# Decode attention with a gated MLP: the output row in two PSUM banks, and the loads of K and wo without the order behind the last round's arm

## The chip, the cores and the metric

The kernel runs on one core of a Trainium2 chip. Five engines work side by side, each with its own queue of instructions: TensorE (PE; its weight loads are shown as PEld), VectorE (DVE), ScalarE (ACT), GpSimd (POOL) and SyncE (SP), which here issues nearly all transfers. Sixteen DMA engines carry the transfers. The metric is the device time of one execution, in microseconds (us).

## The reference

Two sequences, one new token each (`B = 2`, `Sq = 1`, `D = 1024`). `A` is attention with 32 heads over a cache of 16384 positions, `B` a small MLP block, and a gate mixes the two:

```python
g = sigmoid((x * gate_w).sum(-1, keepdims=True))
a = A(x, k_cache, v_cache, wq, wo)   # q = x@wq; softmax(q.k / sqrt(128)); o = p@v; o@wo
b = B(x, w1, w2, w3, w4)             # x1 = x + shifted(gelu(ln(x)@w1))@w2; x1 + gelu(ln(x1)@w3)@w4
return g * a + (1 - g) * b           # B's x is A's x
```

With one token a sequence the shifted parts are all zero, so `x1` is `x`. The caches are bf16, [2, 32, 16384, 128] each: 268 MB of K and 268 MB of V, read once. All the weights together are some 35 MB.

## The kernel before

**Memory.** One big tile `mem` in SBUF has five cells of 4.19 MB. A block of K or V is two heads of one sequence, 8.39 MB, and takes two cells. `K_CELL = (0, 1)`: K of sequence 0 lies in cells 0 and 1, K of sequence 1 in cells 1 and 2, so that the two share cell 1. Therefore `score_first` (four transposes, L423, and their score matmuls, L429) works on the half in cell 1, after which the other sequence's K may be loaded over it, and `score_second` on the other half. V goes to cells 3 and 4 (`V_CELL = 3`), and there is a single place for it. `wo_pair` holds the 256 rows of wo that belong to two heads (0.52 MB).

**Order.** There are 16 pairs of heads. The work on one pair and one sequence `b` is a unit: transposes of K on VectorE (L423), score matmuls (L429), a softmax in two parts (`softmax_a`, `softmax_b`), the product with V (`pv`, L483) and its end (`pv_end`), and after both sequences `project`, which multiplies by `wo_pair` (L375). Units are staggered: the scores of one unit run ahead of the product of the one before. One round of the hardware loop (L600, 15 rounds) is `odd_rest(i)` and then `even_unit(i + 1)`. After it comes an `If` that only the last round takes, with `last_unit`: the last V, the last wo, the last weight w4 in four pieces, and the output.

The loads stand on SyncE in this order in every round: wo (L367) and K of sequence 0 for the next pair (L112), V of sequence 1 (L115), K of sequence 1 (L112), V of sequence 0 (L115). A load is issued when what it overwrites has been read: K of sequence 0 after `score_second(0)` (cell 0) and after `score_first(hp, 1)` (cell 1), the last work on VectorE in a round. The order of instructions within an engine is fixed by `in_order`, which ties each to the one before; waits between engines and on transfers are placed by the tile layer from what reads and writes the same memory, and across the rounds of the loop too. `wo_pair` is read by `project` in `even_unit` and again by `project` in `last_unit`.

**The `If`.** An engine that does not take the arm goes through another one (its rows have L604), in which its semaphores are moved on by as much as the arm would have moved them. Before it adds to a semaphore it waits until that has its value of this round. SyncE's own arm of that kind thus waits for the loads of the round that share semaphores with `last_unit`'s loads; the latest of them is K of sequence 1.

**The output.** All products that end in the output row are added up in one PSUM tile `arow`: quarter `g` of the 1024 columns stands on partitions 32g and 32g + 1, 256 columns wide. Three functions add into it: `mlp_residual` (once, ahead of the loop), `project` (each round) and `mlp_last` (L403, at the very end, four pieces of w4). `write_out` copies quarters 0 and 2 with VectorE (L524) and 1 and 3 with ScalarE (L526) into `out_row`, and SyncE stores it (L527).

Of the kernel before, what the change touches and what calls it, by code (L numbers as in the profile page):

```python
# [10 lines left out]
FP32 = mybir.dt.float32  # L11
# [12 lines left out]
def kernel(  # L24
# [15 lines left out]
    nc = tc.nc  # L40
    P = nc.NUM_PARTITIONS
    B, Sq, D = A_x.shape
    _, H, Sk, Dh = A_k_cache.shape
# [3 lines left out]
    KC = D // P  # L47
# [6 lines left out]
    NJ = 2 * Sk // P  # L54
# [5 lines left out]
    QP = P // Q4  # L60
    CELL = NJ * Dh // 2
    G1 = D // Q4
# [8 lines left out]
    ops = ctx.enter_context(tc.tile_pool(name="ops", bufs=1, space=PSUM))  # L71
# [8 lines left out]
    def region(cell, elements, offset=0):  # L80
        at = cell * CELL + offset
        return mem[:, at : at + elements]
# [21 lines left out]
    K_CELL = (0, 1)  # L104
    V_CELL = 3

    def cache_rows(cache, hp, b):
        two = cache[b, bass.ds(2 * hp, 2)]
        return two.rearrange("h s d -> (h s) d").rearrange("(p j) d -> p (j d)", p=P)

    def load_k(hp, b):
        nc.sync.dma_start(out=region(K_CELL[b], NJ * Dh), in_=cache_rows(A_k_cache, hp, b))  # L112

    def load_v(hp, b, cell=V_CELL):
        nc.sync.dma_start(out=region(cell, NJ * Dh), in_=cache_rows(A_v_cache, hp, b))  # L115
# [6 lines left out]
        out=ident_s[:], in0=ident_f[:], scalar1=-scale, scalar2=None, op0=ALU.mult  # L122
# [10 lines left out]
        out=mask4[:], in_=mask4[:], compare_op=ALU.is_ge, fill=0.0,  # L133
# [3 lines left out]
        out=mask4[:], in_=mask4[:], compare_op=ALU.is_ge, fill=0.0,  # L137
# [11 lines left out]
        out=lmat[:].rearrange("p (g h k) -> p g h k", h=2, k=4),  # L149
        in_=hm2[:].unsqueeze(1).unsqueeze(3).to_broadcast([P, P // 8, 2, 4]),  # L150
# [5 lines left out]
        out=lane[:],  # L156
        in_=ident_f[:].rearrange("p (c k) -> p k c", k=QP),
# [5 lines left out]
    for g in range(Q4):  # L163
        nc.vector.tensor_scalar(
            out=spread[:, g],
# [2 lines left out]
        )  # L168

    oacc = [ops.tile([P, 4 * Dh], FP32, name=f"oacc{k}") for k in range(2)]  # L170
    arow = ops.tile([P, G1], FP32, name="arow")
    S_tiles = [ops.tile([P, GT * QP], FP32, name=f"S{k}") for k in range(2)]
    for t in (oacc[0], oacc[1], arow):
        nc.vector.memset(t[:], 0.0)

    WW = P + NG
# [2 lines left out]
    for k in range(2):  # L179
        t = const.tile([P, 4, WW], BF16, name=f"qw{k}")  # L180
        nc.gpsimd.memset(t[:], 0.0)
        qw.append(t)
        t = const.tile([P, NJ // 4, 2, 4], BF16, name=f"pt{k}")
# [17 lines left out]
    def turned(wide, C):  # L201
        t = mlp.tile([P, C, QP], FP32, tag="turn", name="turn")
        nc.vector.transpose(  # L203
            out=t[:].rearrange("p c k -> p (c k)"), in_=wide.rearrange("p c k -> p (c k)")
        )
        return t[:, :, 0:B]
# [86 lines left out]
    def spread_batch(t, C):  # L293
        return t[:].unsqueeze(1).to_broadcast([P, C, B])
# [31 lines left out]
    for k in range(2):  # L326
        wide = mlp.tile([P, 16, QP], FP32, tag="wide", name="wide")
        nc.scalar.activation(  # L328
            out=wide[:].rearrange("p (c e) i -> p c e i", e=2),
            in_=oacc[k][:].rearrange("p (c i e) -> p c e i", i=QP, e=2),  # L330
            func=ACTF.Copy,
        )
        t = turned(wide[:], 16).rearrange("p (x a v) b -> p a x b v", x=2, a=2)
# [12 lines left out]
    for e in range(2):  # L346
        half = slice(e * HALF, (e + 1) * HALF)
        nc.vector.tensor_copy(
            out=qdu[half].rearrange("p u v -> p (u v)"),
            in_=qdps[half, e].rearrange("p k g n -> p (k g n)"),  # L350
# [13 lines left out]

    def load_wo(hp):
        rows = A_wo[bass.ds(hp * 2 * Dh, 2 * Dh)]
        nc.sync.dma_start(  # L367
            out=wo_pair[:].rearrange("p t n -> p (t n)"),
            in_=rows.rearrange("(p t) n -> p (t n)", p=P),
        )  # L370

    def project():
        for t in range(2):
            for g in range(Q4):
                nc.tensor.matmul(  # L375
                    arow[QP * g : QP * g + B, :],
                    lhsT=oT[:, t, :],
                    rhs=wo_pair[:, t, g * G1 : (g + 1) * G1],
                    start=False,
                    stop=False,  # L380
                    skip_group_check=True,
                )

    def mlp_residual():
        x1g = mlp.tile([P, KC, B], FP32, name="x1g")
        nc.vector.tensor_tensor(
            out=x1g[:], in0=x1T[:], in1=spread_batch(omg, KC), op=ALU.mult
        )
        for r in range(KC):
            for g in range(Q4):  # L390
                nc.tensor.matmul(
                    arow[QP * g : QP * g + B, :].rearrange("b (i r) -> b r i", r=KC)[:, r, :],
                    lhsT=x1g[:, r, :],
                    rhs=ident_f[:, QP * g : QP * (g + 1)],
                    start=(r == 0),
                    stop=False,
                    skip_group_check=True,
                )

    def mlp_last(w4):  # L400
        for r in range(FC):
            for g in range(Q4):
                nc.tensor.matmul(  # L403
                    arow[QP * g : QP * g + B, :],
                    lhsT=h2T[:, r, :],
                    rhs=w4[:, r, g * G1 : (g + 1) * G1],
                    start=False,
                    stop=(r == FC - 1),
                    skip_group_check=True,
                )  # L410
# [29 lines left out]
    def score_first(hp, b):  # L440
        write_qw(hp, b)
        score_chunks(b, halves[1 - b], True, False)

    def score_second(b):
        score_chunks(b, halves[b], False, True)

    def softmax_a(b):
        S = S_tiles[b]
        st = ppool.tile([P, GT, QP], FP32, name="St")
        nc.vector.transpose(out=st[:].rearrange("p j r -> p (j r)"), in_=S[:])  # L450
        m = stat.tile([P, 1], FP32, name="m")
        nc.vector.tensor_reduce(out=m[:], in_=st[:, :, 0:NG], axis=AX.XY, op=ALU.max)  # L452
        Dm = ppool.tile([P, P], FP32, name="Dm")
        nc.scalar.activation(out=Dm[:], in_=ident_s[:], func=ACTF.Copy, scale=m[:, 0:1])  # L454
        st_tiles[b] = (st, Dm)
# [23 lines left out]
    def pv(b, cell=V_CELL):  # L479
        V = view(cell)  # L480
        for g in range(NJ // 4):
            q = g % Q4
            nc.tensor.matmul(  # L483
                oacc[b][QP * q : QP * q + 8, :],
                lhsT=pts[b][:, g].rearrange("p h k -> p (h k)"),
                rhs=V[:, 4 * g : 4 * g + 4, :].rearrange("p j d -> p (j d)"),
                start=(g < Q4),
                stop=(g >= NJ // 4 - Q4),
            )
# [4 lines left out]
    def pv_end(b):  # L494
        osb = ppool.tile([P, 4 * Dh], FP32, name="osb")
        nc.scalar.activation(  # L496
            out=osb[:], in_=oacc[b][:], func=ACTF.Copy, scale=rinvs[b][:, 0:1]
        )
        lines = osb[:].rearrange("p (k d t) -> p k t d", k=4, t=2)
        ot = misc_psum([P, 2])  # L500
        for t in range(2):
            for k in range(4):
                for h in range(2):
                    nc.tensor.matmul(  # L504
                        ot[h * HALF : (h + 1) * HALF, t : t + 1],
                        lhsT=lines[:, k, t, :],
                        rhs=lane[:, k + 4 * h : k + 4 * h + 1],
                        start=(k == 0 and t == 0),
                        stop=(k == 3),
                        skip_group_check=True,  # L510
                    )
        nc.vector.tensor_scalar(  # L512
            out=oT[:, :, b], in0=ot[:], scalar1=g_rep[:, b : b + 1], scalar2=None, op0=ALU.mult
        )
# [4 lines left out]
    def write_out():  # L519
        for g in range(Q4):  # L520
            at = out_row[:, g * G1 : (g + 1) * G1]
            row = arow[QP * g : QP * g + B, :]
            if g % 2 == 0:
                nc.vector.tensor_copy(out=at, in_=row)  # L524
            else:
                nc.scalar.activation(out=at, in_=row, func=ACTF.Copy)  # L526
        nc.sync.dma_start(out=out.rearrange("b s n -> (b s) n"), in_=out_row[:])  # L527


    load_k(0, 0)  # L530
    w3 = load_weight(B_w3, 3)
    compute_gate()
    mlp_residual()


# [6 lines left out]
    softmax_b(0)  # L542
    score_first(0, 1)

    def odd_rest(hp):
        load_wo(hp)
        load_k(hp + 1, 0)
        score_second(1)
        softmax_a(1)
        pv(0)  # L550
        load_v(hp, 1)
        pv_end(0)
        softmax_b(1)

    def even_unit(hp):
        score_first(hp, 0)
        load_k(hp, 1)
        score_second(0)
        softmax_a(0)
        pv(1)  # L560
        load_v(hp, 0)
        pv_end(1)
        project()
        softmax_b(0)
        score_first(hp, 1)
# [34 lines left out]
    with tc.For_i(0, HP - 1, 1, iteration_sync="reg_based") as i:  # L600
# [3 lines left out]
        with tc.If(i >= HP - 2):  # L604
            last_unit(HP - 1)
            in_order()


# [1 line left out]
_INS = ['A_x', 'A_k_cache', 'A_v_cache', 'A_wq', 'A_wo', 'B_x', 'B_w1', 'B_w2', 'B_w3', 'B_w4', 'gate_w']  # L610
# [26 lines left out]
```

## Time and profile before

| | us |
|---|---|
| median of 3 runs | 1337.62 (1336.85 to 1338.44) |
| the profiled execution | 1337.09 |
| its span, first to last instruction | 1334.9 |
| busy: PE / PEld / DVE / ACT / POOL | 772.2 / 335.1 / 652.4 / 130.4 / 12.9 |
| moved by the transfers | 572.68 MB, 429 GB/s over the span |

The page of the profile gives the span, the busy time of each engine and the share of the DMA engines in 40 slices; the trace behind it tells when each instruction ran, what it had waited for, and when transfers were issued. A row of the timeline has the start in us, the duration, the engine and line, the operation, its tiles and how many were merged, and in brackets the idle time before it and what ended that. `SPq`, `PEq` and the like are the queues of the engines, where branches, waits and issues are seen.

### The profile page before, as it was taken

Reading aid. Unit: us, or ns where it says so; the run is one execution under the profiler, and the core shown is the slowest. Engines: PE = TensorE matmul, PEld = TensorE weight load, DVE = VectorE, ACT = ScalarE, POOL = GpSimd, SP = SyncE. Lnnn points to the kernel's source line nnn. Section 1 sums busy time; section 2 is a strip of 40 time slices with the busy share of each in tenths; the row PEclk is TensorE's granted clock in tenths of the full one; section 3 lists DMA queues with packets and bytes.
Section 4 is the critical chain, followed back from the end, with each engine's and each line's share of the span. In section 5 each row is a group of like instructions: output and inputs, shape, how many; then the busy total and the mean of one; then the engine's idle time right before and its main releaser. Section 6 shows DMA issues by size and latency. Waiting matters only on the chain. (4 is left out here: it accounts for less than half of the span.)

```text
span 1334.9 us, 14766 instructions
## 1 busy us (share of the span) xinstructions
PE 772.2 (58%) x5758; PEld 335.1 (25%) x5758; DVE 652.4 (49%) x510; ACT 130.4 (10%) x204; POOL 12.9 (1%) x47
## 2 busy tenths in 40 slices
PE   1554657455566545567555556655556765655763
PEld 1222223222222222222222222222222222222322
DVE  2454455444455544445553445555444555544550
ACT  0011101111110111110011111001111000111110
POOL 1000000000000000000000000000000000000000
PEclk9677878777888777788777788877778876778886
DMA  9999999999999999999999999999999999999997
GB/s 409 436 434 427 438 405 440 416 448 438 426 440 424 440 438 426 438 426 440 424 440 438 426 438 426 440 424 440 438 426 438 426 440 424 440 438 426 438 431 310
DMA packets 13101, 572.68 MB, mean 429 GB/s; under 512 B 1826, under 2 KB 1826, under 8 KB 4004
## 3 DMA queue, kind: packets, MB, share of 16 engines
q1 hardware_dynamic: 12676, 572.53, 99.4%
q8 instruction: 8, 0.13, 0.0%
q10 hardware_dynamic: 416, 0.01, 0.0%
q14 instruction: 1, 0.01, 0.0%
HBM read 572.53 MB, written 0.00 MB: 429 GB/s over the span
## 5 line engine op out<-in xcount | busy, mean ns | idle before, releaser
L429 PE MATMUL S<-KT,qw 128*128 128x512 bf16 x2048 | 554.7, 422 | 356.2 <-DVE KT L423 349.6
L423 DVE STREAM_TRANSPOSE KT<-mem 128x2048 f32<-128x2048 f32 x256 | 573.7, 2286 | 269.6 <-DMA mem<-in_A_k_cache_dram 95.6
L429 PEld LDWEIGHTS <-qw 128*128 128x128 bf16 x2048 | 220.8, 108 | 685.3 <-issue 512.7
L483 PE MATMUL oacc<-mem,pt 128*8 128x512 bf16 x2048 | 117.8, 383 | 8.2 <-DMA mem<-in_A_v_cache_dram 8.2
L454 ACT ACTIVATE Dm<-ident_s,m 128x128 f32<-128x128 f32 x32 | 12.9, 402 | 977.5 <-PE oacc L483 943.6
L467 ACT ACTIVATE pt<-St,nb 64x256 bf16<-64x256 f32 x64 | 89.7, 1402 | 79.4 <-DVE nb L465 78.5
L512 DVE TENSOR_SCALAR oT<-misc,g_rep 128x2 bf16<-128x2 f32 x32 | 7.1, 222 | 166.9 <-PE misc L504 166.9
L476 PE MATMUL misc<-rs,lmat 128*128 128x1 f32 x64 | 18.8, 362 | 106.9 <-ACT pt L467 61.2
L483 PEld LDWEIGHTS <-pt 128*8 128x8 bf16 x2048 | 47.3, 87 | 75.9 <-issue 23.8
L504 PE MATMUL misc<-lane,osb 128*64 128x1 f32 x1024 | 36.1, 199 | 45.3 <-ACT osb L496 45.3
L477 DVE RECIPROCAL rinv<-misc 128x1 f32<-128x1 f32 x32 | 5.4, 169 | 107.5 <-PE misc L476 104.2
L450 DVE STREAM_TRANSPOSE St<-S 128x512 f32<-128x512 f32 x32 | 22.9, 717 | 66.2 <-PE L483 64.2
L504 PEld LDWEIGHTS misc<-lane,osb 128*64 128x64 f32 x1024 | 33.8, 138 | 61.0 <-ACT osb L496 31.7
L476 PEld LDWEIGHTS misc<-rs,lmat 128*128 128x128 f32 x64 | 16.0, 311 | 114.0 <-ACT pt L467 64.7
L496 ACT ACTIVATE osb<-oacc,rinv 128x512 f32<-128x512 f32 x32 | 22.0, 687 | 88.7 <-PE oacc L483 88.7
L467 ACT ACTIVATION_READ_ACCUMULATOR pt<-St,nb 64x1 f32 x64 | 30.5, 477 | 0.0
L465 DVE TENSOR_REDUCE nb<-misc 64x1 f32<-64x64 f32 x64 | 14.2, 222 | 22.0 <-PE misc L460 21.0
L354 POOL TENSOR_TENSOR qw<-qdu,mask 128x16 bf16<-128x16 bf16 x32 | 8.4, 265 | 1181.3 <-PE L483 1109.2
L460 PE MATMUL misc<-Dm,ones_f 128*128 128x128 f32 x64 | 18.7, 380 | 0.0
L452 DVE TENSOR_REDUCE m<-St 128x1 f32<-128x256 f32 x32 | 13.4, 420 | 1.1
L460 PEld LDWEIGHTS misc<-Dm,ones_f 128*128 128x128 f32 x64 | 11.5, 226 | 5.3 <-issue 5.1
L203 DVE STREAM_TRANSPOSE turn<-wide 128x256 f32<-128x256 f32 (+2 forms) x5 | 3.4, 685 | 17.8 <-ACT wide L328 10.4
(80 smaller groups left out, 69.6 us busy)
## 6 DMA issues: line engine op xcount, KB each, us to landing
wo_pair<-in_A_wo_dram SPq DMA_DIRECT2D x16, 512.0 KB, 8.0
mem<-in_B_w_dram SPq DMA_DIRECT2D x1, 7168.0 KB, 31.7
mem<-in_B_w_dram SPq DMA_DIRECT2D x2, 2048.0 KB, 10.0
mem<-in_B_w_dram SPq DMA_DIRECT2D x1, 3840.0 KB, 26.7
mem<-in_B_w_dram SPq DMA_DIRECT2D x1, 1792.0 KB, 30.1
mem<-in_B_w_dram SPq DMA_DIRECT2D x1, 1024.0 KB, 32.1
mem<-in_A_k_cache_dram SPq DMA_DIRECT2D x32, 26.6
mem<-in_A_v_cache_dram SPq DMA_DIRECT2D x32, 31.7
```

Of the source, the lines that this page charges most:

```text
L423: nc.vector.transpose(out=kt[:], in_=Kc.rearrange("p j d -> p (j d)").bitcast(FP32))
L429: nc.tensor.matmul(S, lhsT=qw[b][:, v, NG - 1 - m : NG - 1 - m + P], rhs=ktb[:, half * GT : (half + 1) * GT, w, :, e], start=(first and n ...
L450: nc.vector.transpose(out=st[:].rearrange("p j r -> p (j r)"), in_=S[:])
L452: nc.vector.tensor_reduce(out=m[:], in_=st[:, :, 0:NG], axis=AX.XY, op=ALU.max)
L454: nc.scalar.activation(out=Dm[:], in_=ident_s[:], func=ACTF.Copy, scale=m[:, 0:1])
L460: nc.tensor.matmul(R_ps[:], lhsT=ones_f[:], rhs=Dm[:], start=True, stop=True)
L465: nc.vector.tensor_reduce(out=nb[rows], in_=R_ps[rows, rows], axis=AX.X, op=ALU.min)
L467: nc.scalar.activation(out=pts[b][rows, :, e, :].rearrange("p (m a) k -> p a k m", a=GT // 4), in_=st[rows, :, 0:NG].rearrange("p (a k) m ...
L476: nc.tensor.matmul(tot_ps[:], lhsT=lmat[:], rhs=rs[:], start=True, stop=True)
L483: nc.tensor.matmul(oacc[b][QP * q : QP * q + 8, :], lhsT=pts[b][:, g].rearrange("p h k -> p (h k)"), rhs=V[:, 4 * g : 4 * g + 4, :].rearra ...
L496: nc.scalar.activation(out=osb[:], in_=oacc[b][:], func=ACTF.Copy, scale=rinvs[b][:, 0:1])
L504: nc.tensor.matmul(ot[h * HALF : (h + 1) * HALF, t : t + 1], lhsT=lines[:, k, t, :], rhs=lane[:, k + 4 * h : k + 4 * h + 1], start=(k == 0 ...
```

## The change

The output's PSUM tile becomes two, each in a bank of its own: `arows[0]` has quarters 0 and 1, `arows[1]` quarters 2 and 3, still on partitions 32g and 32g + 1. VectorE copies quarters 0 and 1, ScalarE 2 and 3. One more memset clears the second tile. PSUM has eight banks' worth of tiles afterwards, seven before.

The loads of wo and of K in the loop body are collected in a list, and once the `If`'s instructions exist, each load is declared to have no dependence on any of them across rounds. The list holds three loads: wo, K of sequence 0, K of sequence 1. The loads of V, and those inside `last_unit`, are as before.

```diff
     def load_k(hp, b):
-        nc.sync.dma_start(out=region(K_CELL[b], NJ * Dh), in_=cache_rows(A_k_cache, hp, b))
+        return nc.sync.dma_start(
+            out=region(K_CELL[b], NJ * Dh), in_=cache_rows(A_k_cache, hp, b)
+        )
...
-    arow = ops.tile([P, G1], FP32, name="arow")
+    arows = [ops.tile([P, G1], FP32, name=f"arow{k}") for k in range(2)]
...
-    for t in (oacc[0], oacc[1], arow):
+    for t in (*oacc, *arows):
         nc.vector.memset(t[:], 0.0)
...
     def load_wo(hp):
...
-        nc.sync.dma_start(
+        return nc.sync.dma_start(
...
     # project, mlp_residual, mlp_last: the same edit
-                    arow[QP * g : QP * g + B, :],
+                    arows[g // 2][QP * g : QP * g + B, :],
...
     def write_out():
         for g in range(Q4):
             at = out_row[:, g * G1 : (g + 1) * G1]
-            row = arow[QP * g : QP * g + B, :]
-            if g % 2 == 0:
+            row = arows[g // 2][QP * g : QP * g + B, :]
+            if g < 2:
                 nc.vector.tensor_copy(out=at, in_=row)
             else:
                 nc.scalar.activation(out=at, in_=row, func=ACTF.Copy)
...
+    loads = []
     def odd_rest(hp):
-        load_wo(hp)
-        load_k(hp + 1, 0)
+        loads.append(load_wo(hp))
+        loads.append(load_k(hp + 1, 0))
...
     def even_unit(hp):
         score_first(hp, 0)
-        load_k(hp, 1)
+        loads.append(load_k(hp, 1))
...
         with tc.If(i >= HP - 2):
             last_unit(HP - 1)
             in_order()
+            for load in loads:
+                for ins in nc.cur_bb.bb.instructions:
+                    tc.declare_no_dep(
+                        load.ins, ins, across_iterations=True, reason="last round"
+                    )
```

In the changed kernel the lines stand three to five lower: wo's load at L370, K's at L112, V's at L117, `project` at L378, the copies at L527 and L529, the loop at L605, the `If` at L609.

More of the change, by code (lines that the diff above doesn't have):

```diff
@@ L391, in mlp_residual @@
                 nc.tensor.matmul(
-                    arow[QP * g : QP * g + B, :].rearrange("b (i r) -> b r i", r=KC)[:, r, :],
+                    arows[g // 2][QP * g : QP * g + B, :].rearrange("b (i r) -> b r i", r=KC)[:, r, :],
                     lhsT=x1g[:, r, :],
@@ L403, in mlp_last @@
                 nc.tensor.matmul(
-                    arow[QP * g : QP * g + B, :],
+                    arows[g // 2][QP * g : QP * g + B, :],
                     lhsT=h2T[:, r, :],
```

## The prediction

> **What bounds the kernel now.** I read the page's slices first, then one round of the loop by itself, then SyncE's own waits and the order of its issues, and last the chain that ended last.
>
> The page (section 2: mean busy share of the 16 DMA engines in 40 slices, in tenths; section 3: the queue that SyncE issues on):
>
> ```profile
> DMA  9999999999999999999999999999999999999997
> q1 hardware_dynamic: 12676, 572.53, 99.4%
> ```
>
> One round of the loop, from one issue of wo to the next (columns: busy time of each engine, granted clock, DMA share, GB/s):
>
> ```profile
> 654.50:733.10 78.60, 47.02 (x336) 20.30 (x336) 39.84 (x28) 7.79 (x12) 0.53 (x2) 0.78 1.00 434
> ```
>
> The transfers fill the whole time. In a round of 78.6 us TensorE is busy for 47.0 and VectorE for 39.8, while the DMA share is 1.00 at 434 GB/s. A round moves two K and two V blocks of 8.39 MB each and 0.52 MB of wo, 34.08 MB, and 34.08 MB / 434 GB/s is 78.5 us: the round is as long as its bytes take. Whatever only makes a load start earlier has nothing to fill.
>
> SyncE's waits, over the whole span (us in total, times, longest):
>
> ```profile
> SPq L115 <- PE oacc L483: 234.8, 30, 14.6
> SPq L112 <- DVE KT L423: 170.6, 16, 11.2
> SPq L367 <- PEq L604: 168.4, 14, 16.3
> SPq L604 <- SPq L604: 166.3, 15, 12.5
> ```
>
> SyncE's issues in one round, then the VectorE row at which K for b=1 has landed:
>
> ```profile
> 654.54 0.34 SPq L367 DMA_DIRECT2D wo_pair<-in_A_wo_dram  x1
> 655.30 0.33 SPq L112 DMA_DIRECT2D mem<-in_A_k_cache_dram  x1
> 669.91 0.33 SPq L115 DMA_DIRECT2D mem<-in_A_v_cache_dram  x1
> 692.96 0.33 SPq L112 DMA_DIRECT2D mem<-in_A_k_cache_dram  x1
> 707.77 0.33 SPq L115 DMA_DIRECT2D mem<-in_A_v_cache_dram  x1
> 733.14 0.33 SPq L367 DMA_DIRECT2D wo_pair<-in_A_wo_dram  x1
> ```
>
> ```profile
> 720.48 4.50 DVE L423 STREAM_TRANSPOSE KT<-mem 128x2048 f32<-128x2048 f32 x2 [5.26 <-SPq L604]
> ```
>
> The third wait is the one that the change is after: 168.4 / 14 = 12.0 us a round in which wo's load stands behind TensorE's arm of the `If` (L604). Ahead of it SyncE is held in its own arm (166.3 / 15 = 11.1 us) until K of b=1 has landed, at 720.48; then wo waits on to 733.14. All this is waiting on SyncE and not on the transfers: the page's DMA list has medians from issue to landing of 31.7 us for V and 8.0 us for wo, so V issued at 707.77 is under way to about 739.5, and wo, issued at 733.14, lands at about 741.1. When wo joins the queue it still holds some 6.3 us of work.
>
> The end of the chain that ended last:
>
> ```profile
> 1296.25 32.91 DMA mem<-in_B_w_dram
> 1329.16 0.04 issue
> 1329.20 0.81 PE arow L403 x8
> 1330.03 0.42 DVE out_row L524
> 1330.47 0.38 ACT out_row L526
> 1330.88 0.43 DVE out_row L524
> 1331.33 0.38 ACT out_row L526
> ```
>
> After the last piece of w4 there is a tail of 1334.9 - 1329.16 = 5.7 us, and the four copies stand in it one behind the other, VectorE and ScalarE taking turns.
>
> **The change part by part.** (1) *Loads in the loop.* In the built programs wo's load no longer waits for the semaphore of the last round's wo, and its count of TensorE goes from 934 to 498 (of 1158 a round), that is from the last round's `project` to `even_unit`'s, the matmuls at L375, done at 710.4 in the round shown. So wo goes out as soon as SyncE is through its own arm, at about 720.7 instead of 733.14.
>
> K of b=0, next on SyncE, loses one DMA semaphore. But its count of VectorE is 28 of 41 a round in both programs, the last of the loop body's: the fourth transpose of `score_first(hp, 1)`, which reads the cell that this K overwrites. The row at 720.48 begins those four transposes, and the next one ends them:
>
> ```profile
> 726.45 4.61 DVE L423 STREAM_TRANSPOSE KT<-mem 128x2048 f32<-128x2048 f32 x2 [1.47 <-PE S L429]
> ```
>
> So the stall moves on: wo's 12.0 us behind TensorE become some 10.4 us of K behind VectorE, until 731.06, and K goes out at about 731.2 instead of 733.89: 2.7 us earlier, with 8.3 us of the V block still ahead of it (739.5 - 731.2) instead of 5.6. Nothing else is late by this: SyncE's next load, V, waits as before for `pv` to free its cell (the row at 669.91, a round on), K of b=1 keeps its waits and place, and Pool's rows are the same. Worth: the idle time of the DMA engines that the earlier loads fill, which the round's share of 1.00 puts at 0. The last round's own V and wo take over the two semaphores dropped; they were met rounds before, a few event instructions of 28 ns on a SyncE that waits there anyway. A deeper queue costs nothing seen: at the start SyncE issues 20.97 MB (w1, w2, wq, K) in 3.0 us, more than the 12.5 MB now outstanding (8.3 us of V, wo, K), for a longer issue (0.84 us for the fourth, 0.33 in the loop).
>
> By the Trainium skill (DMA: Bandwidth & Descriptors, "Where 436 GB/s comes from") the 16 ports carry 435.2 GB/s at most, which speaks against a gain from earlier loads; this trace's 434 agrees, and by that figure (an estimate) a round could not go under 78.3 us.
>
> (2) *The copies at the end.* Before: from 1330.03 to 1331.71, 1.68 us in series. After: VectorE copies quarters 0 and 1 from the first bank, ScalarE 2 and 3 from the second, each after TensorE alone. The longer pair is VectorE's, 0.42 + 0.43 = 0.85 us, ScalarE's 0.38 + 0.38 = 0.76. Saved: 1.68 - 0.85 = 0.83 us. VectorE may start up to two matmuls (some 0.15 us) earlier, as its bank is finished first; then ScalarE's pair ends last and 0.9 is saved. SyncE now waits for two engines: one event of about 0.03 us more. I take -0.8; the ends are -0.95 and, if the two banks or the second wait cost what the pairing gives, 0.
>
> (3) *One more memset* of a 128x256 tile on VectorE, 0.27 us by the row of the old one at 6.11 us; VectorE then sits idle for 7.3 us until x lands (13.68). Cost 0; without that cover 0.27 us on a chain to the first w3 load, which is issued at 38.85 while K is under way until 53.6 (2.2 + 51.4, the longest landing at L112).
>
> (4) *Matmuls into two banks.* Same number, shape and order: 8 per round at L375 (0.39 us), under the transfers. Only the last 8 of L403 are in the open (0.81 us); no row shows accumulation alternating between these two, so I bound it by ±0.1 us, from a row's step of 0.1 between eight matmuls, and take 0.
>
> Sum: 0 + (-0.8) + 0 + 0 = -0.8 us. The profiled execution took 1337.09 us (span 1334.9 and 2.2 around it), so it would take 1336.3; it lies 0.5 under the median of three, 1337.62, for which I forecast 1336.8. That is 0.06%, and about 0.2% (2.7 us) is what a measurement of this kernel tells from no change.
>
> **The rivals.** *Slower: the engines serve the later load first.* If K, there at 731.2, were carried ahead of the V that is under way, V would land 19.3 us late (8.39 MB / 434). V's reader has 4.7 us to spare (V at 660.9 by the median, `pv` from 665.6, after its scores), so the next V would be issued 14.6 us later than 669.91, at 684.5, while all that is queued is through at 681.8 (K's row in the round, VectorE starting on it). The engines would stand for 2.7 us and then start from an empty queue, 3.0 us by wo's shortest landing (4.2, less its own 1.2): 5.7 us in 15 rounds, +85 us, 1422. It decides once V is late by more than 4.7 + 681.8 - 669.9 = 16.6 us; an even sharing, 8.3 us late, costs nothing. Against: wo lands 8.0 us after its issue, V's 6.3 and its own 1.2 and little else, so it waited for V's end; at the start K, issued at 2.2, landed 51.4 us later (the longest at L112), the time of all that stood ahead. 3 in 100.
>
> The Trainium skill (DMA: Bandwidth & Descriptors, "Queues, rings and completion order") says that an engine takes descriptors of one ring in order and shares only between queue rows; the trace agrees, since all these loads are on q1.
>
> *Faster: a loss at each seam.* wo's 8.0 us are 0.5 more than 6.3 + 1.2. If that were engines idling between V's end and late-issued loads, it goes in 15 rounds: 7 us, 1330. Against it: the share of 1.00, and the 0.5 lies inside the scatter of medians. 5 in 100.
>
> *The order isn't loosened after all* (another count keeps wo behind the arm): wo stays at 733, the tail still gains, 1336.8 again; 5 in 100, told from the forecast by the trace alone. *The tail gives nothing*, because the release by TensorE or the two waits of the output load eat 0.8 us: 1337.6; 7 in 100.
>
> **How the numbers follow.** The forecast has 80 in 100. With the two cases that end within 0.9 us of it, "within 0.2%" has 80 + 5 + 7 - 1 = 91, faster 5 and slower 3 + 1 = 4 (the 1 for a start of the program that comes out 3 us late). The three runs before lie between 1336.85 and 1338.44, ±0.8 around their median; the sum's bounds are -0.95 to 0.1. So 1336.8 - 0.15 - 0.8 to 1337.7 + 0.8, about 1335.8 to 1338.5; since another median of few runs may sit off by as much again, I give 1335.2 to 1338.8.
>
> **What would show it.** Right: DMA share still 1.00 and 434 GB/s in a round of 78.6 us; wo at L370 issued right after the K of b=1 lands, its wait for PEq gone and its time to landing up from 8 to about 20 us; K (b=0) held by VectorE instead, issued at the end of four transposes, its landing some 3 us longer; VectorE's and ScalarE's copies side by side, the output's issue some 0.9 us after the last matmul instead of 1.7 (1330.0 to 1331.73). Wrong: a round that is not 78.6 us, idle DMA between V and the next load, V (b=0) landing later after its issue than 32 us, or a last piece of w4 that lands more than 1 us off 1329.2.

## The result, and the profile after

| | before | after |
|---|---|---|
| median, same session | 1338.32 us (1336.85 to 1339.49, 13 runs) | 1334.42 us (1334.26 to 1335.73, 13 runs) |
| the profiled execution | 1337.09 | 1334.39 |
| its span | 1334.9 | 1332.2 |
| last piece of w4 landed | 1329.16 | 1327.35 |

The changed kernel takes 0.9973 of the time (95% interval 0.9965 to 0.9981): 3.6 us less by that ratio and 3.9 between the medians, where 0.8 were forecast, and below the range given. In the two profiled executions the difference is 2.7 us, since the one of before lay low in its spread; 0.9 of it lies behind the last transfer and 1.8 ahead of it.

The page after, the slices and SyncE's queue, as before:

```profile
DMA  9999999999999999999999999999999999999997
q1 hardware_dynamic: 12676, 572.53, 99.5%
```

One round after, from wo's issue to the next one:

```profile
641.70:720.40 78.70, 46.96 (x336) 20.24 (x336) 39.80 (x29) 7.79 (x12) 0.54 (x2) 0.78 1.00 433
```

The round is what it was, 78.7 us at 433 GB/s. SyncE's waits after (total, times, longest):

```profile
SPq L112 <- DVE KT L426: 299.7, 30, 11.9
SPq L117 <- PE oacc L486: 238.5, 30, 15.1
...
SPq L609 <- SPq L609: 164.4, 14, 12.5
```

The row of wo behind TensorE's arm (168.4 us, 14 times) is gone, and K behind VectorE now waits twice a round, 30 times. The issues of the same round:

```profile
641.72 0.34 SPq L370 DMA_DIRECT2D wo_pair<-in_A_wo_dram  x1
651.43 0.33 SPq L112 DMA_DIRECT2D mem<-in_A_k_cache_dram  x1
...
720.42 0.33 SPq L370 DMA_DIRECT2D wo_pair<-in_A_wo_dram  x1
```

wo goes out at 720.42 where it went at 733.14, and K follows 9.7 us later. wo's landing, from the view of the tile `wo_pair`, takes that much longer, since it is queued behind V:

```profile
DMA to landing us min/median/max: 9.4/19.6/29.2
```

The end, from the chain of waits and then the timeline:

```profile
1294.99 32.36 DMA mem<-in_B_w_dram
1327.39 0.80 PE arow L406 x8
```

```profile
1328.10 0.86 DVE L527 CAST out_row<-arow 2x256 bf16<-2x256 f32 x2 [10.88 <-PE arow L406]
1328.22 0.78 ACT L529 ACTIVATE out_row<-arow 2x256 bf16<-2x256 f32 x2 [12.48 <-PE arow L406]
1329.04 0.33 SPq L530 DMA_DIRECT2D out_dram<-out_row  x1
```

The copies run side by side: 0.94 us from the first copy to the output's issue, where it was 1.70. (Whether they took turns before because of the shared bank or because the program had them in one tile, no run here separates.) So far everything is as forecast. What was not forecast is that the last piece of w4 lands 1.8 us earlier.

**Where those microseconds are.** The landing of each transfer can be followed in the trace. Up to V of the loop's first round the two kernels agree to 0.2 us. At wo of the next one, the first round that the loop jumps back to (the first looped round from here on), after is 0.9 us ahead. It is 1.1 ahead two rounds later and stays so up to the last V of the loop, from which on it is 1.8 to 2.0 ahead. The windows around that point, first before, then after (columns as above):

```profile
160.00:200.00 40.00, 20.16 (x98) 8.12 (x102) 19.33 (x11) 2.26 (x5) 0.26 (x1) 0.73 0.98 417
```

```profile
160.00:200.00 40.00, 21.47 (x90) 8.36 (x94) 19.34 (x11) 1.40 (x2) 0.26 (x1) 0.71 1.00 431
```

40 us at 14 GB/s less are 0.56 MB, 1.3 us of transfers at 434 GB/s. Before's SyncE issued these two loads there:

```profile
185.92 0.34 SPq L367 DMA_DIRECT2D wo_pair<-in_A_wo_dram  x1
186.69 0.33 SPq L112 DMA_DIRECT2D mem<-in_A_k_cache_dram  x1
```

After's, in the same view:

```profile
169.64 0.34 SPq L370 DMA_DIRECT2D wo_pair<-in_A_wo_dram  x1
179.85 0.33 SPq L112 DMA_DIRECT2D mem<-in_A_k_cache_dram  x1
```

V, the load ahead of them, lands at 187.92 in both kernels, so before issued wo 2.0 us ahead of that (its margin from here on); in the 13 looped rounds that follow the margin is 6.1 to 6.8 us, and after 18.3 in each. wo's landings before, from the view of the tile `wo_pair`, have this one as their shortest:

```profile
DMA to landing us min/median/max: 4.2/8.0/29.8
```

2.0 us is too late. From wo's issue to its first packet pass 0.98 us in the trace, the 16 engines can end their last packets of V (64 KB, 2.42 us each) up to one packet apart (here 1.9 us), and V's landing is shown 0.45 us behind the end of its last packet. To be in every engine's queue before it runs dry wo needs a margin of some 0.98 + 2.42 + 0.45 = 3.9 us, an estimate from these three. Here the engines stood idle for 0.8 us more, in the mean of the 16, than in after's trace (from 176 to 200 us, all packets' time added up).

Why was wo so late there, and only there? It waited for TensorE's way round the last round's arm (L604), one compare-and-branch a round. Before, and then after:

```profile
L604 PEldq COMPARE_BRANCH  x16: 87/227/6551, 179.1 to 1329.2; - x16
```

```profile
L609 PEldq COMPARE_BRANCH  x16: 87/232/5972, 179.7 to 1327.4; - x16
```

The three numbers are min, median and longest in ns: 0.23 us in an ordinary round, 6.55 us the first time, over `last_unit`'s work on TensorE (some 700 rows of matmuls and weight loads in the trace, when the last round runs them). Both kernels pay it (VectorE and TensorE have slack there); only before had a load behind it.

### The profile page after: what moved, and what is told of

The parts are those of the page before. It is cut to its first block, busy times and chain, and to the rows that moved or that the text cites. A ratio compares the mean times of both kernels' runs of the same rounds, so it can differ in the third digit from the quotient of the medians.

```text
span 1332.2 us, 14752 instructions
## 1 busy us (share of the span) xinstructions
PE 777.5 (58%) x5758; PEld 336.7 (25%) x5758; DVE 652.6 (49%) x511; ACT 130.4 (10%) x204; POOL 13.1 (1%) x47
## 6 DMA issues: line engine op xcount, KB each, us to landing
wo_pair<-in_A_wo_dram SPq DMA_DIRECT2D x16, 512.0 KB, 19.6
```

## The experiments

The theory, the seam (S where a letter stands for it): the gain ahead of the tail is this one seam, where SyncE's loads were issued too late to follow V without a gap. Against it: that the second bank does more than shorten the tail, that K's or wo's earlier issue alone carries the gain, and that a little is lost in every round. Edits are against the kernel before unless another is named.

**The banks alone.** `arows` and the pairing in `write_out` as in the change, no `declare_no_dep`.

```diff
-    arow = ops.tile([P, G1], FP32, name="arow")
+    arows = [ops.tile([P, G1], FP32, name=f"arow{k}") for k in range(2)]
...
-            if g % 2 == 0:
+            if g < 2:
```

> The two banks and the copies as changed, the loads ordered behind the arm as before. Theory S (the seam of the first looped round: wo's load stands behind TensorE's first, slow jump over the arm, 6.55 us, and comes when the V ahead of it has all but landed, so the engines run dry): only the tail is gained, 0.85 us under the kernel before, about 1337.4, and the first looped round still shows wo landing 4.2 us after its issue. Rival B (the banks do more than the tail): 2 us or more under the kernel before. Rival K (K's earlier issue in every round brings it): as S.

1337.38 us (11 runs) against 1337.76 for before (33 runs), ratio 0.9995 [0.9986, 1.0004]. The copies are side by side here too:

```profile
1330.73 0.86 DVE L527 CAST out_row<-arow 2x256 bf16<-2x256 f32 x2 [11.13 <-PE arow L406]
```

The tail's 0.8 us can be read in the trace and not in the medians, whose difference is 0.4. The seam is as before: 415 GB/s in 160 to 200 us, wo issued at 185.90. So the banks are not what moved the landing of w4.

**The loads alone.** One `arow` as before, and the declaration for all three loads.

```diff
+            for load in loads:
+                for ins in nc.cur_bb.bb.instructions:
+                    tc.declare_no_dep(
+                        load.ins, ins, across_iterations=True, reason="last round"
+                    )
```

> The loads freed as changed, one bank and alternating copies as before. Theory S: the rest of the gain, 2 to 3 us under the kernel before, about 1335.3, with the spread of the times gone too (before 1336.9 to 1339.5, changed mostly 1334.3 to 1334.5); TensorE's longest jump at the If still 6 us, but wo of that round issued 17 us before. Rival B: nothing or less than 1 us.

1335.36 us (1335.18 to 1335.77, 11 runs), ratio 0.9978 [0.9969, 0.9987]: 2.9 us of the 3.6 by the ratios, 2.4 between the medians. The window has after's rate, and the spread of the times has gone with the seam:

```profile
160.00:200.00 40.00, 21.10 (x90) 8.24 (x94) 19.36 (x12) 2.73 (x4) 0.26 (x1) 0.71 1.00 431
```

**wo alone, K alone.** The same declaration, with only wo, or only the two loads of K, in the list.

```diff
     def odd_rest(hp):
-        load_wo(hp)
+        loads.append(load_wo(hp))
         load_k(hp + 1, 0)
```

> Only wo's load is freed, both loads of K ordered as before; one bank. Theory S: the same as with all three freed, about 1335.3, since K stands behind wo on SyncE and the semaphore that it keeps is moved on by SyncE itself. Rival K: less than half of that gain.

1336.27 us (1336.05 to 1337.42), 0.999 [0.9981, 0.9999]: 1.5 us, between before and the loads together, where the same gain as theirs was expected. SyncE's waits, and its issue of K at the seam:

```profile
SPq L112 <- PEq L608: 32.8, 14, 6.4
```

```profile
186.09 0.33 SPq L112 DMA_DIRECT2D mem<-in_A_k_cache_dram  x1
```

K has a wait of its own for TensorE's arm, which before was hidden behind wo's. wo, issued at 170.04, is 1.2 us of work and covers a part of the gap; K then comes at 186.09, where before it came at 186.69. The window says 421 GB/s, between 417 and 431, in an execution that was the longest of the 11.

```diff
     def odd_rest(hp):
         load_wo(hp)
-        load_k(hp + 1, 0)
+        loads.append(load_k(hp + 1, 0))
```

> Only the two loads of K are freed, wo ordered as before; one bank. Theory S: no gain, about 1338.3, within 0.5 us of the kernel before. Rival K: 2 us or more under it.

1337.47 us (1337.18 to 1338.41), 0.9999 [0.999, 1.0008]: nothing. K stands behind wo on SyncE, and wo still waits:

```profile
SPq L369 <- PEq L608: 167.9, 14, 16.1
```

**How late is too late.** To the changed kernel a few TensorE matmuls that read `wo_pair` are added at the end of the round (2, 10 or 18 of 512 columns), with a result that nothing uses; so wo waits for them in every round.

```diff
+    def hold():
+        H = misc_psum([P, 512])
+        for n in range(2):          # 10, 18
+            nc.tensor.matmul(
+                H[:], lhsT=qw[1][:, 0, 0:P], rhs=wo_pair[:, n % 2, 0:512], start=True, stop=True
+            )
...
         score_first(hp, 1)
+        hold()
```

> The changed kernel, and at the end of each round's body 2 matmuls (128x512) into a spare bank that read the wo tile, so that wo's load must wait for them: it is issued after TensorE's last scores as in the kernel before, but ahead of TensorE's jump over the arm. Theory S: within 0.5 us of the changed kernel, 1334.4, with wo issued some 6 us before V lands in every round, the first looped one included. Rival E (it is the 12 us of earliness in every round that pays): the gain of the loads is gone, 1337 or more.

> The same with 10 matmuls, some 2 us more: wo issued about 4 us before V lands. If the engines need the time from issue to the first packet (1.46 us in the first looped round of the kernel before) and the spread of their last packets (up to one packet of 2.42 us), 3.9 us, this is the edge: 0 to 3 us over the changed kernel. Rival E: as with 2 matmuls.

> The same with 18 matmuls: wo issued about 2 us before V lands, in every round as it was in the first looped round of the kernel before, which lost 1.05 us there. Theory S: some 1 us in each of 15 rounds, 8 to 20 us over the changed kernel, 1342 to 1354. Rival E: no more than 2 us over it.

| matmuls | wo's margin in the looped rounds, us | median us | ratio to before (1337.61) |
|---|---|---|---|
| 2 | 6.5 in the first, 5.7 to 6.8 after it | 1334.79 (10 runs) | 0.9977 [0.9967, 0.9986] |
| 10 | 4.5 in the first, 4.4 to 4.8 after it, once 7.1 | 1336.74 (10 runs) | 0.9994 [0.9984, 1.0003] |
| 18 | 3.0 in the first, 2.4 to 3.8 after it | 1351.23 (4 runs) | 1.0109 [1.0092, 1.0126] |

(Margins are issue to landing in the trace; the 1.46 us in the expectation for 10 matmuls is 0.98 by the trace's own times, and the 0.45 us up to the landing make up for the difference.) wo's landing with 18, in the view of its tile:

```profile
DMA to landing us min/median/max: 4.0/4.5/23.8
```

With 2 matmuls wo is issued at 181.55 in the first looped round, 12 us later than in the changed kernel, and the time is the changed kernel's: an earlier issue than some 6 us is worth nothing. With 18 every round has before's seam, at 16.8 us over the changed kernel, 1.2 at each of the 14 seams. The matmuls do not pay for that themselves: 10 of the 18 cost 2.3 us in all.

With 10 the loss isn't spread over the rounds. In its trace (an execution of 1337.54 us) 0.3 us are lost at the first looped seam and 2.4 at the fourth, where TensorE's jump was long a second time and V, still under way, landed late (hence the 7.1):

```profile
L617 PEldq COMPARE_BRANCH  x16: 87/232/8885, 180.0 to 1330.5; - x16
```

At the other 12, with margins of 4.4 to 4.8 us, at most 0.2 us is lost. With 18 a seam costs 0 to 1.8 us in its trace, 1.1 in the mean. So margins of 2.4 to 3.8 us cost about 1 us a seam, 4.4 and more cost next to nothing, and the 3.9 worked out above lie between.

**The kernel before once more**, for one more trace of its seam.

> The kernel before once more, for a second profile. Theory S: the loss sits in the first looped round again (wo landing about 4 us after its issue there, 8 elsewhere, TensorE's longest jump about 6 us), and a longer execution than 1337.1 shows a longer loss there. Otherwise: the loss is found in other rounds too, or not at all.

1337.96 us in one run. The margin in the first looped round is 2.5 us and 6.0 or more in the others, with 415 GB/s from 160 to 200, and the chain's end has the last w4 piece later than in the first trace:

```profile
1297.38 32.64 DMA mem<-in_B_w_dram
```

It lands at 1297.38 + 32.64 = 1330.02, against 1329.16 in the first profiled execution and 1327.35 after: 2.7 us behind after, where the first trace was 1.8. The gain of the loads alone, 2.4 to 2.9 us, is of the same size.

What these 1.8 and 2.7 us are made of can be worked out from the packets. A landing is that of the latest of the 16 engines. At the last piece of w4 the mean engine of the first trace is 1.4 us behind after's, and it has been so since the round after the seam; in this trace it is 1.8. Of the 1.4 us, 0.8 are idle time and 0.6 are packets that took longer than the usual 2.42 us for 64 KB and 0.16 for 4 KB (up to 2.8 us right behind the seam); of the 1.8, 0.9 and 0.9. The rest is the distance of the latest engine from the mean: 1.3 us in the first trace, 1.7 in this one, 0.8 after. With 18 matmuls the same sum gives 5.7 us of idle time and 9.6 of longer packets, all of the 15.4 us by which w4 lands later there than after.

**A shorter jump.** The kernel before, with most of TensorE's work in the last round's arm left out, and the loads ordered as before.

```diff
     def mlp_last(w4):
-        for r in range(FC):
+        for r in range(FC - 2, FC):
...
-        score_second(1)
+        score_chunks(1, halves[1][:1], False, True)
         softmax_a(1)
-        pv(0)
+        pv(0, groups=4)
...
-        pv(1, V_LAST)
+        pv(1, V_LAST, groups=4)
```

> The kernel before with most of TensorE's work in the last round's arm left out (three of four score chunks, 60 of 64 groups of both products with V, 26 of 28 steps of w4), so that the jump over the arm is 78 rows long on TensorE instead of 580; the loads and their order are as before. Its end is shorter by what is left out, so the first looped round is what counts. If the slow first jump comes from fetching code that lies far ahead: the longest jump at the If falls under 1 us, wo of that round is issued some 6 us before V lands, and its landing takes 7 us or more. If the first pass is slow whatever the distance: 6 us and a landing of 4 us again.

1336.39 us in one run. The jump, now over some 200 rows of TensorE's work instead of 700 (500 fewer, as the expectation's 78 and 580 differ), wo's issue, and the window:

```profile
L604 PEldq COMPARE_BRANCH  x16: 79/224/336, 179.2 to 1327.3; - x16
```

```profile
181.21 0.34 SPq L367 DMA_DIRECT2D wo_pair<-in_A_wo_dram  x1
```

```profile
160.00:200.00 40.00, 23.89 (x164) 10.25 (x164) 19.66 (x12) 3.46 (x6) 0.26 (x1) 0.77 1.00 433
```

wo still waits for TensorE's arm, as before, but the longest jump is 0.34 us instead of 6.55, wo has a margin of 6.8 us in the first looped round, and the gap is gone: 433 GB/s. The last piece of w4 lands at 1327.29, the changed kernel's time (1327.35), without any of the change. That makes the time of that one jump the cause of the seam. Why it is long is told as far as known in the last section.

**The changed kernel again**, in the session of the next experiment.

> The changed kernel once more, on the same chip as its shorter tail: 1334.4, with wo issued 18 us before V lands in all looped rounds and no engine idle at the first seam.

1334.41 us (1334.32 to 1334.82, 8 runs), 0.9971 [0.996, 0.9981] with before at 1338.19.

**A wider copy**, on the changed kernel: each engine copies its two quarters in one instruction of 64 partitions, and the two rows of the output are stored by SyncE and by ScalarE's queue.

```diff
-        for g in range(Q4):
...
+        nc.vector.tensor_copy(out=out_wide[0:HB, :], in_=arows[0][0:HB, :])
+        nc.scalar.activation(out=out_wide[HB:P, :], in_=arows[1][HB:P, :], func=ACTF.Copy)
+        rows = out_wide[:].rearrange("(g k) n -> k g n", k=QP)
+        for b, queue in enumerate((nc.sync, nc.scalar)):
+            queue.dma_start(out=out[b, 0].rearrange("(g n) -> g n", g=Q4), in_=rows[b])
```

> The changed kernel with a shorter tail: one copy for each bank over all its 64 partitions (VectorE the first, ScalarE the second) into a tile [128, 256], and the output stored by two loads' queues, one row each (SyncE and ScalarE). A copy costs by its 256 columns: 0.41 us instead of the pair's 0.86, so 0.4 us under the changed kernel, about 1334.0; if the store from eight places or ScalarE's issue costs as much, the same as the changed kernel.

1392.82 us (1392.0 to 1403.68, 5 runs), 1.0418 [1.0396, 1.044]: 58 us slower than the changed kernel where a gain was expected. SyncE's waits, and one round:

```profile
SPq L608 <- SPq L608: 440.8, 29, 19.7
```

```profile
642.00:721.00 79.00, 42.69 (x322) 18.50 (x320) 35.04 (x27) 7.79 (x12) 0.54 (x2) 0.76 0.97 417
```

SyncE's own way round the arm now waits twice a round. The second store is an eighth transfer in the arm, and with it SyncE's way round the arm waits on one more semaphore, the one that V of sequence 0 counts on (in the changed kernel's trace it does not). So SyncE's skip waits for that V to land, and wo goes out about 1.1 us after the landing in every looped round. That is the seam again, with a negative margin, at about 4 us a round.

**The same with w4 in three pieces**, which takes the arm back to seven transfers.

```diff
-    W4_PIECES = (15, 7, 4, 2)
+    W4_PIECES = (15, 10, 3)
```

> The wide copies and two stores again, with w4 loaded in three pieces (15, 10, 3) instead of four, so that the last round's arm issues eight transfers as... one fewer than with four pieces, and none of them shares a semaphore with V of sequence 0. If the 58 us of the kernel with four pieces come from SyncE's arm waiting for that V (wo issued 1.1 us after it landed, the queue empty): all of them are gone, SyncE's wait in its arm is 11 to 12 us a round again, and the time is within 1 us of the changed kernel, 1333.9 to 1335.4. If they come from the stores or the copies themselves: 1390 again.

1335.43 us (1335.1 to 1336.83, 12 runs), 0.9985 [0.9976, 0.9993] with before at 1337.36. The 58 us are gone with the eighth transfer:

```profile
SPq L608 <- SPq L608: 165.1, 14, 12.1
```

It is still over the changed kernel (1.0 us between medians of different sessions, 1.9 by the ratios). Its timeline, the copies and ScalarE's store:

```profile
1328.59 0.42 DVE L525 CAST out_wide<-arow 64x256 bf16<-64x256 f32 x1 [11.89 <-PE arow L406]
...
1329.12 1.11 ACTq L529 DMA_DIRECT2D out_dram<-out_wide  x1
```

The copies take half as long (0.42 us, where the pair took 0.86), but they begin 0.5 us later than the changed kernel's (1328.10), behind the matmuls of the larger last pieces, and the store takes 1.11 us to issue instead of 0.33.

No version here beats the changed kernel.

## Why the prediction was wrong

It failed at one step, part (1): "Worth: the idle time of the DMA engines that the earlier loads fill, which the round's share of 1.00 puts at 0." The share was read in one round, from 654.5 to 733.1, and taken for all 15. For the rounds like it the 0 holds: with 6.1 to 6.8 us of margin nothing is lost, and the experiment with 2 matmuls shows no difference between some 6 and 18 us. The first looped round is not like it. There wo waited for a jump of 6.55 us, its margin is 2.0 us, the mean engine loses 0.8 us idle and 0.6 in longer packets, and getting that back was worth 2.4 us between the medians, 2.9 by the ratio, in the kernel with the loads alone. The term's measured size is -2.4 to -2.9, where 0 stood.

Two rows that it used said so. The wait of wo behind TensorE had "168.4, 14, 16.3": a mean of 12.0 and a longest of 16.3 for a wait that should be the same each round. And wo's shortest landing, 4.2 us beside a median of 8.0, was taken as the price of a start from an empty queue: it *was* such a start, in this kernel, at 185.92. Both are the same load.

The rival *Faster: a loss at each seam* had the right mechanism and the wrong size: it took 0.5 us from the medians and put it into 15 rounds (7 us, 1330), where it was one round, with its own number. It was argued away with the share of 1.00, which is again the one round's.

Right, step by step. The order: wo goes out once K of b=1 has landed, K is held by VectorE's transposes instead of wo by TensorE, wo's landing takes 19.6 us (about 20), the round is unchanged. After's round lies 1.1 us earlier in its trace (VectorE starts on K of b=1 at 719.37 instead of 720.48); from that start K went out 10.7 us later, as forecast, and wo 1.05 instead of 0.2, with 18.3 us in hand. The later load served first did not happen, and a deeper queue cost nothing. The copies: 1.70 us from first copy to store became 0.94, and the loads alone against the whole change, 1335.36 to 1334.42, give 0.9 between medians of two sessions (0.8 forecast). That the tail's gain shows as only 0.4 between medians in the kernel with the banks alone lies within its interval.

The sum by the measured ratios: loads alone -2.9 us (0.9978), banks alone -0.7 (0.9995), together -3.6, which is what the whole change gave (0.9973, interval -2.5 to -4.7 us). That it fits so closely is partly luck, since each part's interval is more than 1 us wide to either side.

Open: why the packets right behind a seam take longer, and which engine ends up last. The landing of w4 lies 1.8 to 2.7 us behind after's in the traces of before, of which the mean engine explains 1.4 to 1.8. It goes together with the wider spread of before's times (2.6 us, where 9 of after's 13 lie within 0.3).

## What to carry to other kernels

Read the min and the longest of a row beside its mean, and look at the first pass of a loop by itself: one odd round out of 15 is invisible in a slice of the page and in a typical round. For a load that must follow another without a gap, work out how long before the other's landing it is issued, and compare that with its time to the first packet, one packet's time and what passes from the last packet to the landing, in every round. A load whose only tie is to an arm that is not taken inherits what the jump over that arm costs, and one transfer more in that arm can change what every round waits for.

## What the runs showed of the hardware

- The first taken jump over some 700 rows of TensorE's work took 6.55 us (5.8 to 8.2 in the other traces with the whole arm), later ones 0.23 by the median; over some 200 rows the longest was 0.34. In the kernels with 10 and 18 matmuls added a second jump was long too, 8.9 us at 416 us and 8.1 at 260. During the long one a packet of 16 KB of the kind "instruction" runs on one DMA engine for 1.08 us; the kernel before has 8 of these in a run, the kernel with the short arm 5, and none at that place. The Trainium skill (Runtime: NRT & Kernel Launch, "Instruction fetch mechanics") says that a taken branch whose target lies outside the fetched window has to wait for a DMA fetch of it. The trace agrees for the first jump; why the later ones are short, and why one of them was long in two kernels, is not explained by what any run here shows.
- The DMA share of a short window misleads, since a packet counts whole in the window in which it starts. From 182 to 189 us it reads 1.00 in both kernels:

```profile
182.00:189.00 7.00, 0.44 (x2) 0.27 (x3) 2.81 (x2) 0.00 (x0) 0.00 (x0) 0.69 1.00 401
```

  Before moved 401 GB/s there, after 424. From 160 to 200 the shares are 0.98 and 1.00, and those 2% of 40 us are the 0.8 us of idle time. A packet that takes longer than usual counts as busy in either window, so GB/s over a window long against a packet is the column to compare.
- From a load's issue to its first packet 0.98 us passed at the seam, nearly three times the 0.34 us for which SyncE's row shows it issuing.
